# Start-up of a chunked attention followed by a gated MLP: units 0 and 1 from one 512-token load, tiny matmuls first, and a reordered start

## The chip, the core and the metric

The kernel runs on one core of a Trainium2 chip. The metric is the device time of one execution in microseconds; six runs of the kernel before lie within 0.2% of one another (290.04 to 290.66). The granted TensorE clock of each run is given as a share of full speed. Ratios are computed as the mean time of one kernel's fast runs over the mean of the other's in the same rounds, so they are not quite the ratio of the medians quoted here.

## The reference, cut to what matters

```python
# 64-token chunks; q, k, v are (8, 8, 576, 64) fp32
scores = (1 / sqrt(64)) * q_c @ k_c.T                # each chunk attends to itself
attn   = softmax(scores)                             # no mask
x      = (attn @ v_c) as (4608 tokens, 512)          # heads side by side
h      = x @ w_in                                    # 512 -> 2048
g      = h * sigmoid(beta * h)
out    = g @ w_out                                   # 2048 -> 512, fp32
```

## The kernel before

A "unit" is 256 tokens, a "block" two units. TensorE does a unit's scores (64 by 64 chunks, from 32-row tiles, two matmuls each), its PV product and four 128x128 transposes per half unit. Then come the hidden tiles (`hps`, 128 rows of d_ff by 512 tokens, four accumulated matmuls of 128x128 by 512) and the output tiles (`ops`). ScalarE does exp, tanh and copies; VectorE does transposes, normalising and the gate. The start is special: unit 0 is loaded in two halves of four heads, and because nothing else can run yet, "warm" matmuls that compute nothing fill the waits.

```python
for a, eng, dst in ((0, nc.sync, raw0), (1, nc.gpsimd, qk0[1])):    # heads 0-3 fp32, heads 4-7 cast to fp16
    for i, src in enumerate((q, k)):
        eng.dma_start(out=dst[i], in_=src[0, HH*a:HH*a+HH, 0:UNIT, :].rearrange("h (p r) d -> p h r d", r=2))
load_qk(1)                       # unit 1: all heads, cast to fp16
for i in range(4): load_v(i)
...                              # [cut] w_in, w_out, later units
emit_idle(11, 512)               # 11 idle matmuls of 512 columns
emit_T_half(0); emit_sc_half(0)  # transposes on VectorE, scores and exp, heads 0-3
emit_idle(3, 512)
emit_T_half(1); emit_sc_half(1)  # heads 4-7
...
emit_idle(13, 512)
emit_T(1, ("qT", "kT")); emit_sc(1)
emit_idle(4, 512)
emit_pv(0); emit_norm(0, 0); emit_norm(0, 1)
...                              # [cut] transposes, PV of unit 1, idle matmuls between
                                 # four hidden tiles over unit 0's 256 tokens, then over unit 1's
for m in range(4): emit_m(0, m, 256, 256)
for m in range(4, KFF): emit_m(0, m)
```

The softmax here doesn't subtract the row's maximum and nothing guards it: scores larger than these inputs give would overflow.

## Time and profile before

| | kernel before |
|---|---|
| time, median | 290.19 us (six runs, 290.04 to 290.66) |
| TensorE busy | 98% of 288.9 us |
| first hidden tile | 16.13 us |
| first output matmul | 31.37 us |
| granted clock in the records | 1.0 |

The prediction below shows the chain of waits and the loads. These are TensorE's groups in the timeline of the kernel before: start, length, engine, line, operation, count, and in brackets the idle time before it with what ended it.

```profile
7.79 0.45 PE L194 MATMUL sc<-t,t 32*64 32x64 f16 x32 [0.90 <-DVE t L177]
8.17 2.98 PE L362 MATMUL warm<-idle 128*128 128x512 f16 x13
11.08 0.71 PE L231 MATMUL sc<-qT,kT 32*64 32x64 f16 x64
...
12.69 0.56 PE L256 MATMUL x<-vbig,et 64*64 64x65 f16 x32
...
16.13 1.05 PE L313 MATMUL hps<-xt,win 128*128 128x256 f16 x8
```

From 11.08 us TensorE has a short dense passage: scores (64 matmuls in 0.71 us), PV (32 in 0.56 us). Each matmul has its weight load as a second instruction (the page counts 2,715 of each), so 64 matmuls are 128 instructions.

### The profile page before, as it was taken

To read this page: it belongs to the slowest core of one execution; us is meant where nothing else is said; L and a number is where in the kernel's file an instruction comes from. 1 tells how busy PE (TensorE), PEld (TensorE's weight loads), DVE (VectorE), ACT (ScalarE), POOL (GpSimd) and SP (SyncE) were. 2 spreads that over 40 slices of the span, in tenths; PEclk is the share of its full clock that TensorE was granted. 3 is DMA by queue.
4 is the path that set the end of the run, shared out by engine and by line. 5 is a ranking of instruction groups with operands and counts; after the bars stand their busy time and mean duration, and the time that the engine had idled before them with its cause. 6 is when DMAs were issued, how large, how long until landed. Compare 5 with 4: busy or idle time off the path is not lost.

```text
span 288.9 us, 6524 instructions
## 1 busy us (share of the span) xinstructions
PE 282.7 (98%) x2715; PEld 136.0 (47%) x2715; DVE 139.9 (48%) x254; ACT 145.8 (50%) x224; POOL 97.5 (34%) x126
## 2 busy tenths in 40 slices
PE   7999999999999999999999999999999999999995
PEld 2464446545544444444444444444444444444444
DVE  3477444785467544544453444445453636433300
ACT  3277318873566645454545554455445544444411
POOL 8954569387262975070717070000000000000000
PEclk9999999999999999999999999999999999999999
DMA  9999999999979999999999999726363202100112
GB/s 137 169 197 204 180 181 204 218 156 169 166 80 133 196 171 140 164 156 117 172 162 147 142 123 186 109 75 93 91 94 91 75 36 73 39 36 36 39 73 73
DMA packets 142076, 36.86 MB, mean 128 GB/s; under 512 B 130016, under 2 KB 137568, under 8 KB 142048
## 3 DMA queue, kind: packets, MB, share of 16 engines
q0 software_dynamic: 101216, 18.10, 84.2%
q1 hardware_dynamic: 40688, 18.30, 32.7%
q8 instruction: 21, 0.34, 0.5%
q10 hardware_dynamic: 144, 0.07, 0.1%
q14 instruction: 7, 0.06, 0.1%
HBM read 36.71 MB, written 9.44 MB: 160 GB/s over the span
## 4 chain that ended last, share of the span: by engine, by line
PE 94%; DMA 2%; ACT 1%; issue 1%; DVE 1%; POOL 0%; DVEq 0%; ACTq 0%; POOLq 0%
PE hps L313 43%; PE ops L345 42%; PE x L256 2%; DMA h<-in_k_dram 2%; PE warm L362 2%; PE sc L231 2%; PE sc L218 1%; PE ops L552 1%; ACT xt L288 1%; PE xp L287 1%; ACT sg L323 0%; POOL h L370 0%; DVE x L271 0%; DVE t L177 0%; PE xp L295 0%
## 5 line engine op out<-in xcount | busy, mean ns | idle before, releaser
L327 DVE SCALAR_TENSOR_TENSOR gt<-sg,hps 128x512 f16<-128x512 f32 (+1 forms) x153 | 99.1, 654 | 109.3 <-ACT sg L323 109.1
L323 ACT ACTIVATE sg<-hps,beta 128x512 f32<-128x512 f32 (+1 forms) x153 | 100.5, 662 | 74.7 <-PE hps L313 74.7
L313 PE MATMUL hps<-xt,win 128*128 128x512 f16 (+1 forms) x612 | 136.7, 367 | 0.5 <-issue 0.3
L345 PE MATMUL ops<-wout,gt 128*128 128x512 f16 x560 | 131.3, 379 | 0.0
L313 PEld LDWEIGHTS <-win 128*128 128x128 f16 x612 | 58.0, 98 | 61.7 <-issue 1.4
L345 PEld LDWEIGHTS <-gt 128*128 128x128 f16 x560 | 53.7, 98 | 63.0
L355 ACT ACTIVATE osb<-ops 128x512 f32<-128x512 f32 x35 | 20.9, 598 | 42.2 <-PE ops L345 42.2
L110 POOL DMA_DIRECT2D vbig<-in_v_dram x40 | 34.2, 878 | 12.8 <-DMA wout<-in_moe_w_out_dram 4.3
L96 POOL DMA_DIRECT2D qu<-in_q_dram x22 | 18.7, 859 | 40.3 <-DMA qT<-qu 37.5
L271 DVE TENSOR_TENSOR x<-x,rd 128x512 f16<-128x512 f32 (+1 forms) x40 | 25.2, 637 | 1.4
L96 POOL DMA_DIRECT2D ku<-in_k_dram x22 | 18.8, 875 | 0.0
L267 DVE RECIPROCAL rd<-x 128x8 f32<-128x8 f32 x36 | 7.2, 201 | 13.9 <-PE x L256 13.9
L240 ACT ACTIVATE et<-sc 128x1024 f16<-128x1024 f32 (+1 forms) x9 | 7.4, 835 | 11.0 <-PE sc L231 11.0
L362 PE MATMUL warm<-idle 128*128 128x512 f16 x39 | 11.0, 422 | 1.2 <-DVE braw L366 1.2
L224 ACT ACTIVATE et<-sc 128x1024 f16<-128x1024 f32 x10 | 10.1, 1015 | 0.0
L256 PEld LDWEIGHTS <-et 64*64 64x64 f16 x576 | 6.1, 107 | 7.4 <-issue 3.8
L102 POOL DMA_DIRECT2D ku<-in_k_dram x10 | 7.7, 778 | 2.1 <-DMA win<-in_moe_w_in_dram 1.3
L102 POOL DMA_DIRECT2D qu<-in_q_dram x10 | 7.7, 783 | 2.0 <-DMA win<-in_moe_w_in_dram 1.4
L256 PE MATMUL x<-vbig,et 64*64 64x65 f16 x576 | 8.1, 194 | 0.0
L288 ACT COPY xt<-xp 128x512 f16<-128x512 f16 x10 | 5.7, 588 | 3.8 <-PE xp L287 3.8
L154 DVE STREAM_TRANSPOSE kT<-ku 128x512 f32<-128x512 f32 x7 | 4.9, 703 | 3.8 <-DMA ku<-in_k_dram 3.8
L564 DVE TENSOR_SCALAR osb<-ops 128x256 f32<-128x256 f32 (+1 forms) x2 | 0.7, 358 | 12.1 <-PE ops L552 12.1
(37 smaller groups left out, 61.2 us busy)
## 6 DMA issues: line engine op xcount, KB each, us to landing
out_dram<-osb SPq DMA_DIRECT2D x35, 256.0 KB, 4.0
vbig<-in_v_dram POOLq DMA_DIRECT2D x32, 128.0 KB, 8.0
qu<-in_q_dram POOLq DMA_DIRECT2D x20, 128.0 KB, 5.8
ku<-in_k_dram POOLq DMA_DIRECT2D x20, 128.0 KB, 7.7
win<-in_moe_w_in_dram POOLq DMA_DIRECT2D x8, 256.0 KB, 8.9
wout<-in_moe_w_out_dram POOLq DMA_DIRECT2D x4, 512.0 KB, 12.2
qu<-in_q_dram POOLq DMA_DIRECT2D x4, 256.0 KB, 6.7
ku<-in_k_dram POOLq DMA_DIRECT2D x4, 256.0 KB, 7.3
```

The lines of the kernel that those rows point to most:

```text
L96: nc.gpsimd.dma_start(out=tv[off:off + n, sp], in_=src[b, :, s:s + n, :].rearrange("h p d -> p h d"),)
L102: nc.gpsimd.dma_start(out=t[off // 2:(off + n) // 2], in_=src[b, :, s:s + n, :].rearrange("h (p r) d -> p h r d", r=2),)
L110: nc.gpsimd.dma_start(out=vbig[off:off + n, i, :, 0:D], in_=v[b, :, s:s + n, :].rearrange("h p d -> p h d"),)
L224: nc.scalar.activation(out=et, in_=sc, func=ACTF.Exp, scale=scale)
L256: nc.tensor.matmul(out=x[64 * c:64 * c + 64, r, g, 0:D + 1], lhsT=(et[64 * r:64 * r + 64, s, 4 * c + g, :] if u < XU else et[64 * r:64 * r ...
L271: nc.vector.tensor_tensor(out=o, in0=x[:, r, :, 0:D], in1=rd[:, r].to_broadcast(list(o.shape)), op=ALU.mult)
L313: nc.tensor.matmul(out=hps[:, 0:n], lhsT=w_in16[m // 2][:, kk, (m % 2) * 128:(m % 2) * 128 + 128], rhs=xr[:, c0 // CH:(c0 + n) // CH, 2 * ...
L323: nc.scalar.activation(out=sg[:, 0:n], in_=hps[:, 0:n], func=ACTF.Tanh, scale=beta2[:, m:m + 1])
L327: nc.vector.scalar_tensor_tensor(out=gt_t[j][:, m, c0:c0 + n], in0=sg[:, 0:n], scalar=1.0, in1=hps[:, 0:n], op0=ALU.add, op1=ALU.mult,)
L345: nc.tensor.matmul(out=ops, lhsT=gt_t[j][:, kk, t * 128:(t + 1) * 128], rhs=w_out16[kk // 4][:, kk % 4, :], start=(kk == 0), stop=(kk == K ...
L355: nc.scalar.activation(out=osb, in_=ops, func=ACTF.Copy, scale=0.5)
L362: nc.tensor.matmul(out=d[:, 0:w], lhsT=idle[:, 0:128], rhs=idle[:, 0:w])
```

## The change

Its intent is to get unit 1's scores early, from the same load as unit 0's, so that both are ready sooner and hidden tiles can start sooner. Its core, with cuts marked:

```diff
-    raw0 = [const.tile([128, HH, 2, D], FP32, ...          # and qk0, qkT0: 256 tokens
+    tiny = const.tile([128, 64], FP16)
+    raw0 = [const.tile([128, HH, 4, D], FP32, ...          # 512 tokens
...
-            if a == 0 and i == 1: nc.vector.tensor_copy(out=qk0[a][1], in_=raw0[1])
+            if a == 0: nc.scalar.copy(out=qk0[a][i], in_=raw0[i])       # both casts on ScalarE
...
+    def emit_tiny(n):           # 32x64 weights, 8 columns, four positions in turn
...
-                    in_=src[0, ..., 0:UNIT, :].rearrange("h (p r) d -> p h r d", r=2),
+                    in_=src[0, ..., 0:2 * UNIT, :].rearrange("h (p r) d -> p h r d", r=4),
-        load_qk(1)
...
-        emit_idle(11, 512)
+        emit_tiny(63)
+        emit_idle(14, 512)
         emit_T_half(0)
-        emit_sc_half(0)         # [cut: 3 idle, half 1, 13 idle, unit 1, 4 idle, PV of unit 0 ...]
+        emit_sc_half(0, 0); emit_ex_half(0, 0); emit_idle(4, 512, warm)
+        emit_T_half(1)
+        emit_sc_half(0, 1); emit_ex_half(0, 1); emit_sc_half(1, 0); emit_idle(1, 512, warm)
+        emit_pv(0, ("s", "p"))
+        emit_sc_half(1, 1); emit_ex_half(1, 0, 2)
+        emit_norm(0, 0); emit_norm(0, 1); emit_idle(2, 512, warm)
+        emit_xt_pe(0, 0); emit_pv(1, ("x", "p")); ...
-        for m in range(4): emit_m(0, m, 256, 256)
+        for m in range(6): emit_m(0, m, 256, 256)           # six half-width tiles ahead, not four
```

More of the change, by code (lines that the diff above doesn't have):

```diff
@@ L56 @@
     idle = const.tile([128, 512], FP16)
+    tiny = const.tile([128, 64], FP16)
     HH = H // 2
-    raw0 = [const.tile([128, HH, 2, D], FP32, name=f"raw{i}") for i in range(2)]
-    qk0 = [[const.tile([128, HH, 2, D], FP16, name=f"h0{i}{a}") for i in range(2)] for a in range(2)]
-    qkT0 = [[const.tile([128, HH, CH, 2], FP16, name=f"t0{i}{a}") for i in range(2)] for a in range(2)]
+    raw0 = [const.tile([128, HH, 4, D], FP32, name=f"raw{i}") for i in range(2)]
+    qk0 = [[const.tile([128, HH, 4, D], FP16, name=f"h0{i}{a}") for i in range(2)] for a in range(2)]
+    qkT0 = [[const.tile([128, HH, 128, 2], FP16, name=f"t0{i}{a}") for i in range(2)] for a in range(2)]
     braw = const.tile([128, 32], FP32)
@@ L171, in emit_T_half, with emit_sc_half @@
     def emit_T_half(a):
-        if a == 0:
-            nc.scalar.copy(out=qk0[a][0], in_=raw0[0])
         for i in (0, 1):
-            if a == 0 and i == 1:
-                nc.vector.tensor_copy(out=qk0[a][1], in_=raw0[1])
+            if a == 0:
+                nc.scalar.copy(out=qk0[a][i], in_=raw0[i])
             nc.vector.transpose(
                 out=qkT0[a][i].rearrange("p h s e -> p (h s e)").bitcast(FP32).rearrange(
-                    "p (h i r) -> p h r i", h=HH, r=2),
+                    "p (h i r) -> p h r i", h=HH, r=4),
                 in_=qk0[a][i].rearrange("p h r d -> p (h r d)").bitcast(FP32).rearrange(
-                    "p (h r i) -> p h r i", h=HH, r=2),
+                    "p (h r i) -> p h r i", h=HH, r=4),
             )
-    def emit_sc_half(a):
+    def emit_sc_half(u, a):
         if a == 0:
-            et_t[0] = et_p.tile([128, 2, H, CH], FP16, tag="et", name="et")
-            x_t["s0"] = ps_s.tile([128, 2, H, CH], FP32, tag="s", name="sc")
-        sc = x_t["s0"]
+            et_t[u] = et_p.tile([128, 2, H, CH], FP16, tag="et", name="et")
+            pool, tag = ((ps_s, "s"), (ps_x, "x"))[u]
+            x_t["sc", u] = pool.tile([128, 2, H, CH], FP32, tag=tag, name="sc")
+        sc = x_t["sc", u]
         qt, kt = qkT0[a]
@@ L191, in emit_sc_half, with emit_ex_half @@
             for e in range(2):
-                for c in range(4):
-                    p0, o0 = 32 * c, 64 * (c % 2)
-                    nc.tensor.matmul(
-                        out=sc[o0:o0 + 64, c // 2, HH * a + h, :],
-                        lhsT=kt[p0:p0 + 32, h, :, e],
-                        rhs=qt[p0:p0 + 32, h, :, e],
-                        start=(e == 0),
-                        stop=(e == 1),
-                    )
-        hs = slice(HH * a, HH * a + HH)
-        nc.scalar.activation(out=et_t[0][:, :, hs], in_=sc[:, :, hs], func=ACTF.Exp, scale=scale)
+                for s in range(2):
+                    p0 = 64 * u + 32 * s
+                    for c in range(2):
+                        nc.tensor.matmul(
+                            out=sc[64 * c:64 * c + 64, s, HH * a + h, :],
+                            lhsT=kt[p0:p0 + 32, h, 64 * c:64 * c + 64, e],
+                            rhs=qt[p0:p0 + 32, h, 64 * c:64 * c + 64, e],
+                            start=(e == 0),
+                            stop=(e == 1),
+                        )
+    def emit_ex_half(u, a, n=1):
+        hs = slice(HH * a, HH * (a + n))
+        nc.scalar.activation(
+            out=et_t[u][:, :, hs], in_=x_t["sc", u][:, :, hs], func=ACTF.Exp, scale=scale)
     ex_t = {}
@@ L245, in emit_sc, with emit_pv @@
             emit_ex(u)
-    def emit_pv(u):
+    def emit_pv(u, where=("x", "s")):
         et = et_t.pop(u)
@@ L250, in emit_pv @@
             i = 2 * u + s
-            pool, tag = ((ps_x, "x"), (ps_s, "s"))[s]
-            x = pool.tile([128, 2, 4, 128], FP32, tag=tag, name="x")
+            if where[s] == "p":
+                x = [ps_p.tile([128, 4, 128], FP32, tag="p", name=f"y{r}") for r in range(2)]
+            else:
+                pool = {"x": ps_x, "s": ps_s}[where[s]]
+                x = [pool.tile([128, 2, 4, 128], FP32, tag=where[s], name="x")]
             for g in range(4):
@@ L256, in emit_pv @@
                         nc.tensor.matmul(
-                            out=x[64 * c:64 * c + 64, r, g, 0:D + 1],
+                            out=(x[0][64 * c:64 * c + 64, r, g, 0:D + 1] if len(x) == 1 else
+                                 x[r][64 * c:64 * c + 64, g, 0:D + 1]),
                             lhsT=(et[64 * r:64 * r + 64, s, 4 * c + g, :] if u < XU else
@@ L266, in emit_norm @@
         rd = rd_p.tile([128, 2, 4, 1], FP32, tag="rd", name="rd")
-        nc.vector.reciprocal(out=rd, in_=x[:, :, :, D:D + 1])
         x16 = x_p.tile([128, 2, 4, D], FP16, tag="x16", name="x16")
-        for r in ([0, 1] if u < 2 else [slice(0, 2)]):
+        for r, z in [(slice(0, 2), x[0])] if len(x) == 1 else list(enumerate(x)):
+            nc.vector.reciprocal(out=rd[:, r], in_=z[..., D:D + 1])
             o = x16[:, r]
             nc.vector.tensor_tensor(
-                out=o, in0=x[:, r, :, 0:D], in1=rd[:, r].to_broadcast(list(o.shape)), op=ALU.mult
+                out=o, in0=z[..., 0:D], in1=rd[:, r].to_broadcast(list(o.shape)), op=ALU.mult
             )
@@ L283, in emit_xt_pe @@
         xf = x16_t.pop((u, s)).rearrange("p r h d -> p (r h d)")
-        pool, tag = (ps_x, "x") if s == 0 else (ps_s, "s") if u == 2 else (ps_p, "p")
-        xp = pool.tile([128, 4, 128], FP16, tag=tag, name="xp")
+        tag = "s" if u < 2 else "xp"[s]
+        xp = {"x": ps_x, "s": ps_s, "p": ps_p}[tag].tile([128, 4, 128], FP16, tag=tag, name="xp")
         for g in range(4):
@@ L357, in emit_t, with idle_bank, emit_idle @@
         nc.sync.dma_start(out=out[r0:r0 + 128, :], in_=osb)
-    def emit_idle(n, w):
-        d = ps_p.tile([128, 512], FP32, tag="p", name="warm")
+    def idle_bank():
+        return ps_p.tile([128, 512], FP32, tag="p", name="warm")
+    def emit_idle(n, w, d=None):
+        d = idle_bank() if d is None else d
         for _ in range(n):
             nc.tensor.matmul(out=d[:, 0:w], lhsT=idle[:, 0:128], rhs=idle[:, 0:w])
+    def emit_tiny(n):
+        d = [ps_p.tile([128, 512], FP32, tag="p", name="tiny") for _ in range(2)]
+        for i in range(n):
+            c = i % 4
+            p0, o0 = 32 * c, 64 * (c % 2)
+            nc.tensor.matmul(
+                out=d[c // 2][o0:o0 + 64, 0:8],
+                lhsT=tiny[p0:p0 + 32, :],
+                rhs=tiny[p0:p0 + 32, 0:8],
+            )
     with tc.manual_schedule():
+        nc.vector.memset(tiny, 0.0)
         nc.vector.memset(idle, 0.0)
@@ L371 @@
                     out=dst[i],
-                    in_=src[0, HH * a:HH * a + HH, 0:UNIT, :].rearrange("h (p r) d -> p h r d", r=2),
+                    in_=src[0, HH * a:HH * a + HH, 0:2 * UNIT, :].rearrange("h (p r) d -> p h r d", r=4),
                 )
@@ L388 @@
         loads_to(3)
-        emit_idle(11, 512)
+        emit_tiny(63)
+        emit_idle(14, 512)
         emit_T_half(0)
-        emit_sc_half(0)
-        emit_idle(3, 512)
+        emit_sc_half(0, 0)
+        emit_ex_half(0, 0)
+        warm = idle_bank()
+        emit_idle(4, 512, warm)
         emit_T_half(1)
-        emit_sc_half(1)
         nc.vector.transpose(out=bt, in_=braw)
-        nc.scalar.activation(out=beta2, in_=bt[:, 0:KFF], func=ACTF.Copy, scale=0.5)
-        loads_to(4)
-        emit_idle(13, 512)
-        emit_T(1, ("qT", "kT"))
-        emit_sc(1)
+        emit_sc_half(0, 1)
+        emit_ex_half(0, 1)
+        emit_sc_half(1, 0)
+        emit_idle(1, 512, warm)
         loads_to(5)
-        emit_idle(4, 512)
-        emit_pv(0)
+        emit_pv(0, ("s", "p"))
+        emit_sc_half(1, 1)
+        emit_ex_half(1, 0, 2)
         emit_norm(0, 0)
         emit_norm(0, 1)
-        emit_idle(3, 512)
+        emit_idle(2, 512, warm)
         emit_xt_pe(0, 0)
-        emit_idle(3, 512)
+        emit_pv(1, ("x", "p"))
+        emit_norm(1, 1)
+        emit_norm(1, 0)
+        nc.scalar.activation(out=beta2, in_=bt[:, 0:KFF], func=ACTF.Copy, scale=0.5)
         emit_xt_pe(0, 1)
-        emit_idle(2, 512)
-        emit_pv(1)
-        emit_norm(1, 0)
-        emit_norm(1, 1)
-        a0, v0 = emit_m(0, 0, 0, 256, True)
-        a1, v1 = emit_m(0, 1, 0, 256, True)
-        a0()
-        a1()
-        emit_xt_pe(1, 0)
-        v0()
-        v1()
-        a0, v0 = emit_m(0, 2, 0, 256, True)
-        a0()
-        emit_xt_pe(1, 1)
-        v0()
-        emit_m(0, 3, 0, 256)
-        for m in range(4):
+        d = [emit_m(0, m, 0, 256, True) for m in (0, 1)]
+        d[0][0]()
+        emit_xt_pe(1, 1)
+        d[1][0]()
+        d += [emit_m(0, m, 0, 256, True) for m in (2, 3)]
+        d[2][0]()
+        emit_xt_pe(1, 0)
+        d[3][0]()
+        for _, vec in d:
+            vec()
+        for m in (4, 5):
+            emit_m(0, m, 0, 256)
+        for m in range(6):
             emit_m(0, m, 256, 256)
-        for m in range(4, KFF):
+        for m in range(6, KFF):
             emit_m(0, m)
```

## The prediction

The forecast came to 29.05 us for the first output matmul, 2.3 us less than before, of which it took 2.2: 288.1 us. h k at 8.4 us is 8.8 less 0.7 for longer runs and plus 0.3 for the longer raw loads in the other queue. The 0.3 was a guess of mine; the kernel after shows only that GpSimd's first q/k packet came at 5.02 us with the raw loads doubled, at 3.67 before. Where the text says that w_in is served behind everything else: in the kernel before its first packet (512 bytes) ran at 12.03 us, the last one of q and k (256 bytes) at 9.84. For the 63 tiny matmuls' "estimate 1 us" the nearest measured figure is 64 score matmuls in 0.71 us.

> **What bounds the kernel now.** I read the page first, then the chain of waits in order of time, then the timeline of the first 20 us, then the DMA view and the table of stretches. The page says who is full:
>
> ```profile
> PE 282.7 (98%) x2715; PEld 136.0 (47%) x2715; DVE 139.9 (48%) x254; ACT 145.8 (50%) x224; POOL 97.5 (34%) x126
> ```
>
> TensorE is busy 98% of a 288.9 us span (290.27 us as timed). But busy is not useful: the group "warm<-idle" has 39 matmuls that compute nothing. So the useful reading is the chain of waits (start, length, what):
>
> ```profile
> 2.13 5.14 DMA h<-in_k_dram
> ...
> 7.79 0.45 PE sc L194 x32
> 8.24 2.91 PE warm L362 x13
> 11.15 0.64 PE sc L231 x64
> ...
> 12.76 0.28 PE x L256 x16
> ...
> 16.84 0.84 ACT sg L323 x2
> 17.69 0.52 ACT xt L288
> 18.20 0.23 ACT sg L323
> ...
> 18.47 0.60 ACT xt L288
> ...
> 19.11 12.27 PE hps L313 x64
> 31.37 6.91 PE ops L345 x32
> ```
>
> From 19.11 us on there is a nearly unbroken stream of large matmuls to the end. In front stands a start-up that is latency, not work: loads, scores, exp, PV, normalising, transposing, one after another. Useful matmuls in those 19.1 us add up to about 4.8 us (scores 0.45+0.45+0.64, PV 2 x 0.38, transposes 16 at 0.055, sixteen 256-wide hidden matmuls at 0.119); some 14 us are filler and waiting. The change touches only the start-up, so its value is how much earlier the first output matmul (31.37) comes; I read nothing behind it that would change that shift.
>
> What feeds the start-up are these transfers (KB each, us from issue to landing):
>
> ```profile
> raw<-in_q_dram SPq DMA_DIRECT2D x1, 256.0 KB, 3.0
> raw<-in_k_dram SPq DMA_DIRECT2D x1, 256.0 KB, 3.2
> qu<-in_q_dram POOLq DMA_DIRECT2D x1, 256.0 KB, 5.9
> ku<-in_k_dram POOLq DMA_DIRECT2D x1, 256.0 KB, 6.4
> h<-in_q_dram POOLq DMA_DIRECT2D x1, 128.0 KB, 5.3
> h<-in_k_dram POOLq DMA_DIRECT2D x1, 128.0 KB, 5.1
> ```
>
> With the issue times of the timeline (0.74, 1.26, 2.86, 3.73, 1.24, 2.13) they land at 3.7, 4.5, 8.8, 10.1, 6.5 and 7.2 us. Unit 1's scores start at 11.08, after ku has landed (10.1) and been transposed (0.71).
>
> [...]the granted-clock row reads 1.0 throughout: weight loads of the idle matmuls are 0.43 us apart from 1.60 to 3.73 us and three fall within 0.53 us from 4.08.
>
> ```profile
> 3.31 0.15 PEld L362 LDWEIGHTS <-idle 128*128 128x128 f16 x1 [0.28 <-issue]
> 3.73 0.15 PEld L362 LDWEIGHTS <-idle 128*128 128x128 f16 x1 [0.28 <-issue]
> 4.08 0.53 PEld L362 LDWEIGHTS <-idle 128*128 128x128 f16 x3 [0.20 <-issue]
> ```
>
> [...](last two columns: DMA share, GB/s written): 165 GB/s while q/k come as 256-byte writes, 196 while w_in comes as 512-byte writes.
>
> ```profile
> 6.00:7.00 1.00, 0.89 (x22) 0.24 (x7) 0.43 (x1) 0.60 (x1) 1.00 (x2) 1.00 1.68 165
> 14.00:22.00 8.00, 7.74 (x92) 5.28 (x92) 5.88 (x18) 5.72 (x13) 4.32 (x7) 1.00 1.45 196
> ```
>
> [...]
>
> **The change part by part.**
> *Loads.* The four q/k loads become 512 tokens long: raw (fp32, SyncE) 512 KB each, h (cast to fp16, GpSimd) 256 KB each, runs twice as long, same number of runs; unit 1's own two loads and their 1.8 us of GpSimd issue vanish. Raw: between 3 and 4 us the page of stretches shows 292 GB/s, so 256 KB more is +0.9 us and 512 KB more +1.75 us at that rate, somewhat less with longer runs: raw q at 4.3, raw k at 5.9 (estimates). h: its k tile is now the last of 512 KB in the cast queue, exactly where qu is today (8.8 us); longer runs (x 165/196 on some 4.5 us) save 0.7[...]. Estimate 8.4 us.
> *First score half.* Both casts now on ScalarE, 1024 columns each; the 1024-wide exp takes 1.02 us, so q 4.3-5.3, k 5.9-6.9. A 512-column VectorE transpose takes 0.71: k done at 7.6. Score half 0 at 7.7 (before: 5.69). Idle work ahead of it, 63 tiny matmuls (estimate 1 us) and 14 wide, half of them at 0.43, ends at about 6 to 7, so it delays nothing.
> *Second half.* VectorE transposes h q at 7.6-8.3, h k at 8.4-9.1. Scores (unit 0, half 1) at 9.2, exp 0.60 after 0.5: PV of unit 0 at P = 10.3. Before it was 12.69. Unit 1's scores need no further load, and the v tiles move up by the same 2 us or more.
> *From PV to the first hidden tile.* PV 0.45, score half 0.45, then one exp of 1024 columns: ScalarE busy P+0.95 to P+2.0. Copy of the first transposed tile to P+2.6, beta scale 0.21, copy of the second P+2.95 to P+3.55. First hidden tile at P+3.6 = 13.9 (before 16.13). VectorE meanwhile: norms of 0.85 (wide) and 1.2 us (two banks) in turn, the last at P+4.45, no longer than ScalarE's line.
> *From there to the output matmuls.* Twelve 256-wide half tiles: 48 matmuls at 0.119 (12.27 less 48 at 0.216, over 16) = 5.7; ten full tiles 40 x 0.216 = 8.6; two transposes 0.45; a wait of about 0.4 since a half tile costs ScalarE 0.47 and VectorE 0.42 against TensorE's 0.475, so that the four buffers barely turn over. Sum 15.15: output matmuls at P+18.75 = 29.05. Two more half tiles than before cost 8 x (2 x 0.119 - 0.216) = 0.2, already inside.
> *Sum.* 31.37 - 29.05 = 2.3 us less, of which I take 2.2: 290.27 - 2.2 = 288.1 us, 0.8%. Filler removed (39 wide down to 21 wide and 63 tiny) is not a gain of its own: it lies in waits.
>
> **The rivals.**
> *The doubled first load takes the gain back.* If raw k is last served among 2 MB of loads (fp32) and lands at 7 rather than 5.9, half 0's transposes finish at 8.8, push those of h to 10.3, and P becomes 11.5: 289.3. [...]Against it: SyncE's packets start near 1.9 us and GpSimd's land no sooner than 6.5.
> *Weights become the wait.* w_in's first tile lands 15.63 - just ahead of its use at 16.13 today, since its issue at 8.79 plus 6.8 us is served behind everything else. With about 2.7 us less in front, it comes at 13; tile 3's pair is needed at P+6, some 16.3, against about 15.6. If the DMA queue did not speed up, PE would wait there and the gain would be under 0.7 us: 289.7. The six half tiles are there to use two more weight tiles before unit 1 is ready.
> *ScalarE becomes the start-up's bound.* It now has both casts, the 1024-wide exp, four copies and six tanh of 0.47 in one line. If a copy falls behind two tanh, as the chain shows today at 16.84-19.06, another 0.5 to 1 us goes: 288.8.
> *The clock.* [...]the half clock lasts to 6 or 7 us; the filler ends up to 1 us later, at about 7.7, still within the wait. Worth 0 to 0.3 us.
> *Better than thought.* If long runs bring h k at 7.5, VectorE's transposes bind at 8.9 and P is 10.0; with no buffer wait, 287.3.
>
> **Range and chances.** The rivals span 287.3 to 289.7 around 288.1, and most are estimates of 0.5 to 1 us in landing times: 8 in 10 for 286.9 to 289.5. Faster by 2% would need 5.8 us, which means P at 6.7 us, when h k cannot have landed: 0.02. Slower by 2% needs a stall of 8 us in the stream: 0.01. Within 2%: 0.97.
>
> **What would show it.** h k landing near 8.4, and raw k near 5.9; first score half near 7.7, second near 9.2; PV of unit 0 near 10.3; first hidden matmul near 13.9; first output matmul near 29, with no new gap over 0.5 us on TensorE after 14; after that the same timeline shifted by 2.2 us, with the same end of 2.5 to 3 us of stores. Wrong if hps waits for win, if raw k rather than h k opens the chain, or if the shift at 29 us is lost before the end.

## The result, and the profile after

The changed kernel takes 294.48 us (median of six, 293.63 to 295.84) against 290.19: a ratio of 1.0152, 95% interval 1.0123 to 1.0180. That is 4.3 us longer where 2.1 us less had been forecast. All six runs show a mean granted clock of 0.983 to 0.988, where the kernel before shows 0.998 to 1.000 (in its runs beside the experiments below).

The whole loss is in front of the first output matmul. In the chain of waits of the kernel after:

```profile
11.80 3.14 issue
14.94 0.48 PE sc L195 x13
...
24.67 10.98 PE hps L321 x60
35.65 6.91 PE ops L353 x32
```

The first output matmul comes at 35.65 us, 4.28 later than before (31.37), which is the difference in time. And 3.14 us of the chain are "issue": time in which TensorE waited for nothing that the profile shows. The timeline of TensorE and its weight loads shows where:

```profile
9.96 0.71 PE L195 MATMUL sc<-t,t 32*64 32x64 f16 x64 [0.43 <-DVE bt L420]
...
11.12 0.32 PE L263 MATMUL x<-vbig,et 64*64 64x65 f16 x16
11.25 0.32 PE L263 MATMUL y<-vbig,et 64*64 64x65 f16 x16
11.49 0.20 PEld L195 LDWEIGHTS <-t 32*64 32x64 f16 x14
11.50 0.31 PE L195 MATMUL sc<-t,t 32*64 32x64 f16 x13
14.94 0.48 PE L195 MATMUL sc<-t,t 32*64 32x64 f16 x19 [3.14 <-issue]
...
18.74 1.87 PE L321 MATMUL hps<-xt,win 128*128 128x256 f16 x8 [0.67 <-ACT xt L296]
```

Unit 1's second group of 32 score matmuls stops after 13 and goes on 3.14 us later. All 32 have the same inputs and the same output tile, so by the program a data dependency should have held back the first, not the fourteenth. Now count: up to 11.80 us TensorE had done 63 tiny, 14 wide, 32 score, 4 wide, 64 score, 1 wide and 32 PV matmuls with their weight loads (420 instructions), then 13 matmuls and 14 weight loads, and two further instructions that stand in the records (a drain and a semaphore wait): **449**.

A second thing changed. In the stretches of the kernel after (first the stretch and its length; the last three numbers are the granted clock, DMA share and GB/s), the clock halves inside the gap, at 13.2 us, and stays so until 23.4 us:

```profile
12.00:13.00 1.00, 0.00 (x0) 0.00 (x0) 0.97 (x4) 0.00 (x0) 0.91 (x2) 1.00 1.46 205
13.00:14.00 1.00, 0.00 (x0) 0.00 (x0) 0.48 (x2) 0.00 (x0) 0.00 (x1) 0.59 1.42 189
14.00:15.00 1.00, 0.06 (x5) 0.06 (x8) 0.00 (x0) 0.00 (x0) 0.12 (x1) 0.50 1.47 197
```

So there are two losses: the gap, and half-speed matmuls after it (the first eight hidden matmuls take 1.87 us, in t75 1.03). From the gap's end to the first hidden tile 3.80 us pass (14.94 to 18.74), and from there to the first output matmul 16.91. The same stretches take 3.0 and 14.95 us where there is no gap and a full clock (t75 below). Gap 3.14, plus 0.8, plus 1.96: 5.9 us.

### The profile page after: what moved, and what is told of

Read it like the earlier page. It is cut to its first block, busy times and chain, and to the rows that moved or that the text cites. A ratio compares the mean times of both kernels' runs of the same rounds, so it can differ in the third digit from the quotient of the medians.

```text
span 292.8 us, 6631 instructions
## 1 busy us (share of the span) xinstructions
PE 283.5 (97%) x2768; PEld 138.9 (47%) x2768; DVE 140.8 (48%) x254; ACT 147.6 (50%) x227; POOL 95.6 (33%) x124
## 4 chain that ended last, share of the span: by engine, by line
PE 93%; DMA 2%; ACT 1%; issue 1%; DVE 1%; SPq 0%; DVEq 0%
PE hps L321 44%; PE ops L353 42%; PE x L263 2%; DMA raw<-in_k_dram 2%; PE sc L235 1%; PE sc L222 1%; PE ops L575 1%; DVE t L176 1%; PE xp L295 1%; ACT xt L296 1%; PE sc L195 0%; ACT h L175 0%; PE warm L373 0%; ACT et L205 0%; SPq L393 0%
## 5 line engine op out<-in xcount | busy, mean ns | idle before, releaser
L321 PE MATMUL hps<-xt,win 128*128 128x512 f16 (+1 forms) x620 | 138.7, 368 | 0.8 <-ACT xt L296 0.7
L321 PEld LDWEIGHTS <-win 128*128 128x128 f16 x620 | 59.8, 99 | 61.7 <-issue 1.3
L97 POOL DMA_DIRECT2D qu<-in_q_dram x22 | 18.7, 857 | 48.2 <-DMA qT<-qu 38.3
L279 DVE TENSOR_TENSOR x<-x,rd 128x512 f16<-128x512 f32 x34 | 23.5, 691 | 1.3
L97 POOL DMA_DIRECT2D ku<-in_k_dram x22 | 18.7, 874 | 0.0
L244 ACT ACTIVATE et<-sc 128x1024 f16<-128x1024 f32 (+1 forms) x8 | 6.4, 811 | 8.3 <-PE sc L235 8.2
L373 PE MATMUL warm<-idle 128*128 128x512 f16 x21 | 7.8, 529 | 0.0
L103 POOL DMA_DIRECT2D ku<-in_k_dram x9 | 6.8, 758 | 2.2 <-DMA win<-in_moe_w_in_dram 1.4
L103 POOL DMA_DIRECT2D qu<-in_q_dram x9 | 6.8, 767 | 2.0 <-DMA win<-in_moe_w_in_dram 1.3
L195 PE MATMUL sc<-t,t 32*64 32x64 f16 x128 | 1.9, 201 | 4.4 <-issue 3.1
```

The lines of the kernel that those rows point to most:

```text
L97: nc.gpsimd.dma_start(out=tv[off:off + n, sp], in_=src[b, :, s:s + n, :].rearrange("h p d -> p h d"),)
L103: nc.gpsimd.dma_start(out=t[off // 2:(off + n) // 2], in_=src[b, :, s:s + n, :].rearrange("h (p r) d -> p h r d", r=2),)
L279: nc.vector.tensor_tensor(out=o, in0=z[..., 0:D], in1=rd[:, r].to_broadcast(list(o.shape)), op=ALU.mult)
L321: nc.tensor.matmul(out=hps[:, 0:n], lhsT=w_in16[m // 2][:, kk, (m % 2) * 128:(m % 2) * 128 + 128], rhs=xr[:, c0 // CH:(c0 + n) // CH, 2 * ...
```

## The experiments

**The theory (A).** TensorE ran out of instructions. That is my reading; no view shows it directly. The DMA part of both profiles has a queue that it calls "instruction":

```profile
q8 instruction: 21, 0.34, 0.5%
```

It carries 21 packets of 16 KB in each of the two kernels. TensorE has 5,464 and 5,571 recorded instructions there, so if the packets are TensorE's, one holds some 260 of them (an estimate: 5,464 / 21 = 260, 5,571 / 21 = 265). Run t75 below, whose only change is 24 more TensorE instructions, has 22. In the kernel after, the window from 12.5 to 12.6 us holds one of them:

```profile
q8 instruction: 1, 0.02, 59.2%
```

The packet's own record runs from 12.53 to 13.48 us, inside the gap, and TensorE goes on at 14.94. I call the place after the 449th instruction an edge; run b113 below has a gap 256 instructions further on. In the kernel after the last 256 instructions in front of the edge pass in 3.5 us, from 8.27 to 11.80, since they are almost all small score and PV matmuls. In the kernel before, the first packet ran at 12.11 us, and its 449th instruction did not start before 15.87. When a packet is asked for, no trace shows. What such a packet brings is called a block.

**Rival B.** A hidden data or PSUM-bank wait in unit 1's scores. **Rival C.** A packet only comes when its instructions are missing, so that every edge costs 3 us. A further question is what the clock costs by itself.

### Tiny matmuls alone: 95, none, and other instructions in their place

```diff
-        emit_tiny(63)
+        emit_tiny(95)              # run t95
+        emit_tiny(0)               # run t00
-        emit_idle(14, 512)
+        emit_idle(45, 160)         # run w45 (63 tiny kept)
```

> 95 tiny matmuls instead of 63: 64 more TensorE instructions at the very start, some 0.4 us, nothing else. Theory A (the instruction supply: TensorE ran dry at its 449th instruction[...]): [...]the 3.1 us gap and the half clock after it vanish, and the time is 287 to 289 us. Theory B (a hidden data or bank wait of unit 1's second score half): gap unchanged in the same score group, 294 to 295 us. Theory C (fetched only on demand): a gap of about 3.1 us moves 64 instructions earlier in the program, into unit 1's first score half, about 10.4 us; 293 to 295 us.

> No tiny matmuls: 126 TensorE instructions fewer at the start. Theory A: [...]no gap in unit 1's scores, a gap of 0 to 3 us at the first hidden tiles; 288 to 293 us. Theory B: gap stays in unit 1's second score half, 294 us. Theory C: a gap of about 3.1 us at the first hidden tiles, 292 to 294 us.

> 63 tiny kept, but the first 14 wide idle matmuls of 512 columns become 45 of 160 columns: about the same busy time (7200 for 7168 columns), 62 instructions more. Theory A: it is the count that matters, so as with 95 tiny: no gap, 287 to 289 us. If it were the tiny ones' shape or time on the array that matters, the gap stays: 294 us.

Measured: t95 291.79 us (ratio 1.0039, 0.9992 to 1.0085), t00 290.98 (1.0018, 0.9990 to 1.0046), w45 289.47 in one run, whose state is therefore unknown (the kernel before: 290.25).

With 95 tiny matmuls there is no gap at all: more idle instructions, 2.7 us less. The 45 narrower idle matmuls, with the same 63 tiny and nearly the same busy time, do the same, so it is the count that matters and not the tiny shape. And with no tiny matmuls the gap does not vanish but moves, to the inside of the first hidden tile. In TensorE's timeline of t00:

```profile
14.59 0.27 PE L321 MATMUL hps<-xt,win 128*128 128x256 f16 x1 [0.67 <-ACT xt L296]
16.57 1.22 PE L321 MATMUL hps<-xt,win 128*128 128x256 f16 x5 [1.71 <-issue]
```

By the records that is again after the **449th** instruction, a different matmul on different data. Rival B is out: the gap follows the count. Rival C is out too: t95 and w45 pass their 449th instruction without a gap. In t00 the packet ran from 14.02 to 14.91 and TensorE went on at 16.57.

The time of t95 is not as forecast, and its stretches say why. There is no gap, yet the clock is halved from 12.4 us on:

```profile
12.00:13.00 1.00, 1.00 (x65) 0.87 (x65) 0.67 (x2) 0.05 (x1) 0.91 (x2) 0.69 1.49 193
13.00:14.00 1.00, 1.00 (x6) 0.44 (x4) 0.93 (x5) 0.98 (x1) 0.84 (x2) 0.50 1.44 196
```

Three of its four runs have a clock of 0.988 and take 291.6 to 292.6 us; the one at 1.0 takes 289.31. So the half clock alone is worth some 2.7 us here (three runs against one).

The clock records of the traces give the times of its changes. It fell 6.83 us after it had risen and stayed down for 10.24 in the kernel after; the two times are 6.83 and 6.83 in t95, 6.83 and 10.24 in t72, and 10.24 and 3.41 in t00. The mean clock fits: 10.24 us at 0.50 in a span of 292.8 take 0.0175 from it, and the profiled run of the kernel after has 0.983. What makes the clock fall is not shown. In the kernel after it fell at 13.19 us, 1.39 after TensorE had stopped; in t95 it fell near 12.4, with scores and PV running and no gap on TensorE longer than 1.17 us after the first scores. And the clock first rises at another time in each execution, from 3.99 us (before) to 9.97 (g1). Whether this decides which runs of t95, t75 and v1 lose their clock, no run shows.

### Where the edge lies: 72 and 75 tiny, and a fuller wait

```diff
-        emit_tiny(63)
+        emit_tiny(72)              # run t72
+        emit_tiny(75)              # run t75; f75 has also emit_idle(6, 512, warm) for emit_idle(4, 512, warm)
```

> The changed kernel with 72 tiny in place of 63, 18 instructions more. Theory A[...]: [...]the block is usable at 11 to 12, needed at 11.5: gap 0 to 0.6 us in place of 3.1; 288 to 290. Theory B: unchanged, 294.

> 75 tiny, 24 instructions more than the changed kernel. Theory A: [...]no gap; and the block's packet comes at 7.5 to 8.4, behind most of the h loads, so that they land at 8.6 to 9.2 and not at 9.6 as with 95. 288 to 289.5 if the clock holds.

> 75 tiny and six instead of four wide idle matmuls between the two score halves of unit 0. As with 75, but less idle TensorE time ahead of 10 us. If the half clock without a gap (as with 95 tiny, from 12.7 us) comes from too little TensorE work between 8 and 12 us, the clock stays at 1.0 in all runs and the time is 288 to 289[...].

Measured: t72 294.54 us (1.0147, 1.0126 to 1.0168), t75 289.52 (0.9990, 0.9956 to 1.0025), f75 289.65 (0.9989, 0.9966 to 1.0013).

Three tiny matmuls, six instructions that take less than 0.1 us, are worth 5 us. In t72 the gap is there, now after the fourth matmul of the group instead of the thirteenth, because 18 more instructions stand in front; again the 449th:

```profile
11.47 0.22 PE L195 MATMUL sc<-t,t 32*64 32x64 f16 x4
14.69 0.58 PE L195 MATMUL sc<-t,t 32*64 32x64 f16 x28 [3.00 <-issue]
```

In t75 the same group runs through:

```profile
12.34 0.45 PE L195 MATMUL sc<-t,t 32*64 32x64 f16 x32
```

The packet ran at 12.28 us with 72 and at 5.53 us with 75. My forecast for 72 (gap nearly gone) was wrong. That for 75 was right but for the packet's time and, with it, the landing of h k (9.65 us, not 8.6 to 9.2). It is not a slide but a switch: with six instructions more the packet ran 6.75 us earlier, in one profiled execution of each. What sets the packet's time is not shown.

In t75 one run of four had a clock of 0.987 and took 291.55 us; the other three, at 1.0, took 289.30 to 289.64. That is the cleanest price of the half clock: the same kernel, about 2.1 us, though from a single run. f75, at 289.22 to 290.58 us slower than the forecast 288 to 289, had no clock below 0.999, but four runs against one in four do not show that its two more idle matmuls are the reason.

### The same in the kernel before

```diff
-        emit_idle(11, 512)
+        emit_tiny(30)              # run b30; b113 has 113. Both on the kernel BEFORE
+        emit_idle(9, 512)
```

> The kernel BEFORE with 30 tiny matmuls and 9 instead of 11 wide ones in front: 56 TensorE instructions more, no useful work changed. Theory A (instruction supply[...]): [...]the 449th falls just behind unit 0's PV at about 13.2. A new gap of 0.5 to 1.5 us exactly there, where before has none; 290.5 to 292. Theory B (the changed kernel's own data or bank waits): no gap, 290.2.

> The kernel BEFORE, with 113 tiny and 9 instead of 11 wide ones in front: 222 TensorE instructions more, no useful work changed (run b30 had put the edge where the block was ready in time, and so told nothing). Theory A: [...]the 705th falls in unit 1's PV near 16.2. Expect a gap of 1 to 2 us after the 705th instruction, in or just behind PV of unit 1, that before does not have, and 291 to 293 us. Theory B: no gap there.

Measured: b30 291.05 us and b113 291.06 in one run each, of unknown state (before: 290.31 and 290.43); only their traces are used. b30 showed no gap. That is a miss of mine: I had put its 449th instruction at 13.2 us, but the edge stands in front of the second pair of the first transpose group, which has to wait for VectorE until 14.29 anyway, and the packet ended at 12.84, 1.45 before that. It told nothing. b113 put a later edge, the 705th, behind unit 1's PV. There a gap appears that the kernel before does not have, inside an accumulated tile, after its first matmul:

```profile
16.15 0.45 PE L257 MATMUL x<-vbig,et 64*64 64x65 f16 x32
16.53 0.28 PE L314 MATMUL hps<-xt,win 128*128 128x256 f16 x1
17.09 0.94 PE L314 MATMUL hps<-xt,win 128*128 128x256 f16 x7 [0.28 <-issue]
```

By the records this is after the **705th** instruction, 449 plus 256, and in a kernel that has none of the change's data flow. The gap is smaller than forecast (0.28 us idle for 1 to 2); the packet ran at 14.63 us.

### Moving the packet, and four tiles ahead in place of six

In the kernels whose packet runs early, h k (the load of k for heads 4 to 7 into tile h) lands later: 9.61 us in t95 and 9.65 in t75, against 8.64 in the kernel after and 8.61 in t00. These runs try to put the packet between the loads and the need.

```diff
-        emit_tiny(63)
-        emit_idle(14, 512)
+        emit_tiny(20); emit_idle(8, 512); emit_tiny(60); emit_idle(6, 512)    # run g1, with 5 idle between the halves
+                                                                           # run g4: g1 with range(4) for the tiles ahead
+        emit_tiny(63); emit_idle(4, 512); emit_idle(34, 160)                  # run v1
```

> The changed kernel with its idle start cut up: 20 tiny, 8 wide, 60 tiny, 6 wide in place of 63 tiny and 14 wide (34 more instructions), and 5 wide instead of 4 between the score halves. Aim: [...]its packet runs at 8 to 9 us, behind the h loads and ahead of the need at 11.4. Theory A: no gap, h k lands at 8.6 to 8.8 (not 9.6), first hidden tile near 14.6, 288.2 to 288.8 us in runs with the clock at 1.0, some 2 us more in those where it drops. If the packet of 16 KB is not what delays h k with 75 and 95 tiny, h k lands near 9.6 all the same and the time is 289.4.

> As the run before it, with four half-width hidden tiles ahead of unit 1 as in the kernel before, in place of six. If the two more tiles cover the wait for unit 1's transposed tiles, TensorE waits 0.3 to 0.9 us at the first full tile and the time is that much longer; if they do not matter, the times are the same to 0.2 us.

> The changed kernel with 4 wide and 34 of 160 columns in place of 14 wide (48 instructions more)[...]. Theory A: no gap or one under 0.5 us; h k at 8.6 to 9.8; 288.5 to 289.5 us with the clock at 1.0.

> The kernel of run w45 again, timed: 289.2 to 289.6 us in runs with the clock at 1.0, 0.2 to 0.4% under the kernel before; if its clock drops in some runs, these are 2 us longer.

| run | packet at | gap | h k lands | first hidden tile | first output matmul | time, median | ratio to before (95%) |
|---|---|---|---|---|---|---|---|
| before | 12.11 | none | | 16.13 | 31.37 | 290.19 | |
| after | 12.53 | 3.14 | 8.64 | 18.74 | 35.65 | 294.48 | 1.0152 (1.0123 to 1.0180) |
| t00 | 14.02 | 1.71 | 8.61 | 14.59 | 32.80 | 290.98 | 1.0018 (0.9990 to 1.0046) |
| t75 | 5.53 | none | 9.65 | 15.46 | 30.41 | 289.52 | 0.9990 (0.9956 to 1.0025) |
| g1 | 10.51 | 0.74 | 8.78 | 16.21 | 31.16 | 289.48 | 0.9970 (0.9957 to 0.9984) |
| g4 | 9.06 | none | 9.39 | 15.20 | 30.61 | 289.63 | 0.9981 (0.9967 to 0.9995) |
| v1 | 8.44 | none | 9.33 | 15.14 | 30.09 | 289.24 | 0.9969 (0.9943 to 0.9996) |
| w45b | 6.77 | none | 9.40 | 15.21 | 30.16 | 289.44 | 0.9968 (0.9954 to 0.9983) |

(Middle columns are of the profiled run.) g1 missed its aim: its packet came at 10.51 us, and a gap of 0.74 us is back, inside unit 0's PV and after the 449th instruction once more:

```profile
11.92 0.28 PE L263 MATMUL y<-vbig,et 64*64 64x65 f16 x11
12.94 0.23 PE L263 MATMUL y<-vbig,et 64*64 64x65 f16 x5 [0.74 <-issue]
```

This is one execution, and chance has a part in it: g4 has the same instructions up to here, and its packet came at 9.06 us. In g1's execution the clock rose only at 9.97 us (g4: 4.74), so six wide idle matmuls took 2.74 us in place of 1.47, and TensorE came to its first scores at 8.41 us in place of 8.06. The profiled run is also the slowest of g1's five (290.05 us; the fastest took 288.93), and no trace of the others was kept.

With the four other gaps the figures are these: from the packet's end to TensorE's next instruction it is 1.46 us (after), 1.66 (t00), 1.47 (t72), 1.48 (g1) and 1.52 (b113).

g4 tells what the two more half tiles are worth. With four ahead TensorE waits for unit 1's transposed tile:

```profile
18.34 3.85 PE L321 MATMUL hps<-xt,win 128*128 128x256 f16 x25 [0.79 <-ACT xt L296]
```

From first hidden tile to first output matmul g4 takes 15.41 us and v1, w45b and t75 14.95: six ahead saves 0.46. The timed runs do not settle it: g1 and g4 differ by 0.15 us, and their intervals overlap. But g1, gap and all, also takes 14.95 us for this stretch, so the profiles agree.

w45b, timed in six runs with clocks of 0.999 to 1.0, beats both kernels: 289.44 us, 0.3% under the kernel before and some 5 us under the kernel after, with nothing changed but 14 idle matmuls of 512 columns cut into 45 of 160. v1 is as good in the mean and had runs from 288.47 to 291.26, the latter with a clock of 0.994.

**What stays open.** In no run are h k early (8.6 to 8.8) and the gap absent together. In t95, t75, f75 (9.51), w45 (9.83), w45b, v1 and g4, all with a packet before 9.1 us, h k landed at 9.3 to 9.8; in after, t00, t72 (8.77) and g1, all with a later one, at 8.6 to 8.8. So an early packet goes with a load 0.6 to 1.2 us later. That the packet holds the load up is not shown: in g4 h q landed at 8.03, late, before the packet's record begins. It is also not shown what makes the clock fall without a gap in some runs of t95, t75 and v1.

## Why the prediction was wrong

The step that failed is unit 1's second score half, in the part from PV to the first hidden tile: "PV 0.45, score half 0.45". It ran from 11.50 to 15.42 us, 3.9 us for 0.45, and 3.14 of them are the gap, in which TensorE waited for nothing that the profile shows. Behind it stands what I wrote of the idle work in front, "so it delays nothing". I counted the tiny matmuls as time ("estimate 1 us", measured 1.02). They were 126 instructions, and they moved the 449th instruction into the passage where the change had packed its smallest matmuls most densely. The dense passage matters by itself: without any tiny matmuls (t00) there is a gap too, of 1.71 us. The durations in the sum also took a full clock for granted, and half clock after the gap cost another 2.8 us (0.8 and 1.96).

Among the rivals none was a shortage of instructions, and the clock rival was about its opening at the start, priced at 0 to 0.3 us; its falling again was not considered. The part behind the start-up held: "I read nothing behind it that would change that shift", and the 4.28 us at the first output matmul are the 4.29 of the time.

Point by point:
- **Loads.** Right. Raw q and k at 4.3 and 5.9 us; measured 4.57 and 5.88. h k at 8.4; measured 8.64. The first rival (a doubled load takes the gain back) did not come about. But in the kernels without a gap h k landed at 9.3 to 9.8. In w45b this load opens the chain of waits, and the first output matmul comes at 30.16, 1.2 us ahead of the kernel before and not 2.3.
- **Transposes.** Mis-sized. I took 0.71 us from the kernel before; with four rows in place of two in the pattern each took 1.06 to 1.12 us, for the same 512 columns. (That the pattern is the reason is not shown: no run changed it alone.) In the form "count: shortest/median/longest in ns":

```profile
L176 DVE STREAM_TRANSPOSE t<-h x4: 1057/1076/1121, 5.7 to 8.8; 128x512 f32<-128x512 f32 x4
```

  That is why the score halves came at 8.12 and 9.96 us and not at 7.7 and 9.2, and PV at 11.12 and not at 10.3.
- **From PV to the first hidden tile.** Right where no gap stands in it: 3.6 forecast, 3.5 in t00 (11.10 to 14.59).
- **From there to the output matmuls.** Right: 15.15 forecast, 14.95 in t75, w45b and v1. Two more tiles ahead are worth 0.46 us there (g4).
- **Weights and ScalarE as rivals.** Neither became the wait: in w45b, v1 and t75 nothing on TensorE waits for win. ScalarE's copy of the second transposed tile is waited for 0.67 us, as worked out.
- **The clock at the start.** It rose at 6.36 us in the kernel after (before: 3.99), and the idle work ended at 7.29 us, later than the 6 to 7 forecast but still inside the wait until 8.12. Whether the tiny matmuls were the reason is not shown.
- **A slip.** The useful matmuls of the start add up to 5.1 us by the terms given, not 4.8. Nothing rests on it.
- **The sum.** With t00's first hidden tile (14.59, clock still full) and 14.95 behind it, the first output matmul would come at 29.54: 1.8 us ahead of the kernel before, an estimate close to the forecast 2.2. From there to the measured 35.65 are 6.1 us, and gap and half clock account for 5.9. So the sign of the forecast shift was right for the work, and what the forecast lacked was 5.9 us of another kind.

## What to carry to other kernels

Count instructions as well as microseconds where many small matmuls stand together: here 256 instructions passed in 3.5 us, and TensorE then stood for 3.14. Filler counts too. If "issue" stands in the chain in the middle of a group of equal matmuls, count from the start, and see whether the gap follows the count when idle instructions in front are added or taken away, as it did in t72 and t00. The cheapest cure here was a few more idle instructions early (three tiny matmuls were worth 5 us); fewer and larger instructions in the dense part were not tried. And look at the granted clock behind every new gap of some microseconds: here it nearly doubled the cost, with 2.8 us beside 3.14.
